# Turning x on VectorE instead of TensorE, in quarter rows with four fetches per tile: lightning attention followed by a mixture of experts

## The chip, the cores and the metric

One core of one Trainium2 chip. The metric is the device time of one execution, in microseconds (us), as a median over executions. The experiments ran in five calls; all kernels of one call ran on the same chip, beside fresh runs of the kernel before.

## The reference, cut to what matters

```python
# attention: B=4, H=8 heads, S=768, D=64, blocks of 64 tokens, decay lam per head
for b in range(nb):
    intra = einsum('bhic,bhjc->bhij', qb, kb) * Dmask;  intra = einsum('bhij,bhjd->bhid', intra, vb)
    inter = einsum('bhid,bhde->bhie', qb * lam_pow, kv_state)
    out[:, :, sl] = intra + inter
    kv_state = lam_block * kv_state + einsum('bhsd,bhse->bhde', kb * rev_pow, vb)
x = out.transpose(0, 2, 1, 3).reshape(B, S, 512)
# experts: E=8, hidden F=1024
for each sequence b, token s:
    fresh_e = argmax(x[b, s] @ w_gate)
    e = fresh_e if s == 0 or local_gate[b, s] < 0.5 else prev_e        # locality
    out[b, s] = softmax(logits)[e] * (relu(x[b, s] @ w1[e]) @ w2[e])
```

Which expert a token takes is known only after its attention, and depends on the tokens before it. So the kernel makes x, routes the 3072 tokens, gathers them by expert into tiles of 128, and runs two matrix products per tile.

## The kernel before

There are 24 attention steps (128 tokens each, numbered 0 to 23), then 24 expert tiles (0 to 23) and some half tiles. Attention leaves x with the features on the partitions (`xc`). The kernel gathers it by token from memory, where it lies with one row per token, and multiplies it by `w1` with the features on the partitions again. So x is turned twice, both times by TensorE, against an identity matrix:

```python
def rows_of(s):                                   # once per attention step
    px = pg.tile([P, DM], F32, name="pk1")
    for a in range(A):                            # A = 4
        nc.tensor.transpose(px[:, P*a:P*a + P], xc[:, a, ORDER[s][0]], ident)
    xn = moe.tile([P, DM], F32, name="xn")
    nc.scalar.copy(xn, px)
    nc.scalar.dma_start(out=x_dram[P*s:P*s + P, :], in_=xn)

def collect(xg, i, j):                            # one tile's 128 tokens, by index: ONE transfer of 256 KB
    nc.gpsimd.indirect_dma_start(out=xg, in_=x_dram[:n, :],
        in_offset=bass.IndirectOffsetOnAxis(ap=gidx[i][:, j:j + 1], axis=0), ...)

def turned(g):                                    # once per expert tile
    pt = pg.tile([P, DT, P], F32, name="po1")
    for d in range(DT):                           # DT = 4
        nc.tensor.transpose(pt[:, d], xgt[g % 2][:, P*d:P*d + P], ident)
    nc.vector.tensor_copy(xtt[g % 2], pt)

def hidden(g, half):                              # 32 matmuls, then one relu on ScalarE
    ...
    nc.scalar.activation(hts[g][:, FT//2*half:FT//2*half + FT//2], ph, ACT.Relu)

# the order of tile 3 (finished(g) is output(g), written(g), weights(g + 2))
        hidden(3, 0)
        hidden(3, 1)
        by_slots(1, (0, 1, 2, 3, 4))              # routing of the later tiles, small matmuls
        turned(4)
        finished(3)
```

`xgt` has two buffers. `written(g)` scales the output on VectorE and scatters it by an indirect transfer that GpSimd issues too, so GpSimd has two transfers per tile. The routing (`fresh_experts` ... `by_slots`) is cut into stages, hung into the attention steps from 9 on (`extras`) and into tiles 0 to 3. The program has TensorE, VectorE and SyncE run in exactly the order written (`tc.manual_schedule(engines={PE, DVE, SP})`).

## Time and profile before

| | value | how to read it |
|---|---|---|
| time | 494.96 us (494.44 to 497.23) | three runs |
| span of the profiled execution | 493.0 us | first to last instruction of the core |
| attention, to the first expert matmul | 106.9 us | timeline: where tile 0's first matmul starts |
| one plain expert tile | 14.45 us | distance of two tiles' first matmuls |
| GpSimd | 106.8 us (22%) | busy time in the page |
| last tile's start to the end | 23.0 us | second product, the last output's scatter and its landing |

A plain tile is 14.45 us of TensorE with nothing between. The attention stage is mixed: there TensorE, VectorE and the loads are all busy for more than half of the time.

### The profile page before, as it was taken

Reading aid. Unit: us, or ns where it says so; the run is one execution under the profiler, and the core shown is the slowest. Engines: PE = TensorE matmul, PEld = TensorE weight load, DVE = VectorE, ACT = ScalarE, POOL = GpSimd, SP = SyncE. Lnnn points to the kernel's source line nnn. Section 1 sums busy time; section 2 is a strip of 40 time slices with the busy share of each in tenths; the row PEclk is TensorE's granted clock in tenths of the full one; section 3 lists DMA queues with packets and bytes.
Section 4 is the critical chain, followed back from the end, with each engine's and each line's share of the span. In section 5 each row is a group of like instructions: output and inputs, shape, how many; then the busy total and the mean of one; then the engine's idle time right before and its main releaser. Section 6 shows DMA issues by size and latency. Waiting matters only on the chain. (4 is left out here: it accounts for less than half of the span.)

```text
span 493.0 us, 10193 instructions
## 1 busy us (share of the span) xinstructions
PE 475.2 (96%) x4231; PEld 351.6 (71%) x4231; DVE 127.3 (26%) x315; ACT 84.7 (17%) x212; POOL 106.8 (22%) x118
## 2 busy tenths in 40 slices
PE   6999999989999999999999999999999999999992
PEld 5877788776777667658657856876667777666770
DVE  6645677652367301011010101101110110110000
ACT  2256656331110000000000001000000000000000
POOL 5575564300101300221011100201101101110000
PEclk9899999999999999999999999999999999999997
DMA  7999999996788999999999997699954980894000
GB/s 272 411 418 380 352 342 330 401 368 233 260 319 292 324 378 399 395 376 397 398 333 386 398 398 277 211 330 319 327 194 157 310 314 31 284 332 169 23 25 17
DMA packets 49850, 146.42 MB, mean 297 GB/s; under 512 B 3244, under 2 KB 3244, under 8 KB 46960
## 3 DMA queue, kind: packets, MB, share of 16 engines
q1 hardware_dynamic: 42096, 125.86, 69.9%
q0 software_dynamic: 4224, 13.37, 7.1%
q10 hardware_dynamic: 3456, 6.29, 3.4%
q8 instruction: 36, 0.59, 0.5%
q14 instruction: 38, 0.31, 0.2%
HBM read 153.90 MB, written 12.98 MB: 338 GB/s over the span
## 5 line engine op out<-in xcount | busy, mean ns | idle before, releaser
L646 PEld LDWEIGHTS ps<-xt,w 128*128 128x128 f32 x1536 | 175.0, 192 | 14.0 <-issue 12.9
L646 PE MATMUL ps<-xt,w 128*128 128x128 f32 x1536 | 177.1, 276 | 0.8 <-DVE xt L631 0.8
L653 PE MATMUL pk<-w,ht 128*128 128x512 f32 x384 | 168.8, 592 | 0.0
L653 PEld LDWEIGHTS pk<-w,ht 128*128 128x128 f32 x384 | 71.1, 190 | 80.4 <-issue 80.4
L648 ACT ACTIVATE ht<-ps 128x512 f32<-128x512 f32 x48 | 28.7, 598 | 314.7 <-PE ps L646 314.2
L659 POOL DMA_INDIRECT out_dram<-y,sidx x24 | 24.6, 1026 | 196.3 <-DVE y L658 179.3
L658 DVE TENSOR_SCALAR y<-pk,gate 128x512 f32<-128x512 f32 x24 | 18.0, 751 | 146.0 <-PE pk L653 140.6
L637 DVE COPY xt<-po 128x512 f32<-128x512 f32 x23 | 15.9, 691 | 143.2 <-PE po L636 143.1
L621 POOL DMA_INDIRECT xg<-x_dram,gidx x24 | 25.0, 1041 | 121.2 <-PE po L636 84.1
L189 DVE TENSOR_TENSOR sm<-ps,mask 128x512 f32<-128x512 f32 x46 | 29.6, 685 | 15.1 <-PE ps L185 15.0
L165 POOL TENSOR_TENSOR qd<-inp,lamq 128x512 f32<-128x512 f32 x20 | 25.6, 1282 | 23.3 <-PE po L212 8.8
L185 PE MATMUL ps<-inp 64*64 64x128 f32 x736 | 26.3, 282 | 2.0 <-DMA inp<-in_qkv_dram 2.0
L225 PE MATMUL po<-sm,inp 128*64 128x128 f32 x384 | 26.9, 284 | 0.3 <-DMA inp<-in_qkv_dram 0.3
L225 PEld LDWEIGHTS po<-sm,inp 128*64 128x64 f32 x384 | 21.1, 140 | 7.5 <-issue 6.6
L168 POOL TENSOR_TENSOR kd<-inp,rev 128x512 f32<-128x512 f32 x20 | 22.4, 1122 | 16.1 <-PE pk L234 7.6
L185 PEld LDWEIGHTS ps<-inp 64*64 64x64 f32 x736 | 20.6, 136 | 5.6 <-issue 4.6
L246 ACT COPY xn<-pk 128x512 f32<-128x512 f32 x24 | 14.1, 588 | 30.6 <-DMA x_dram<-xn 19.8
L216 ACT ACTIVATE kv<-kv,lamq 128x64 f32<-128x64 f32 x64 | 17.1, 337 | 9.8 <-PE po L212 6.4
L228 ACT COPY xc<-po 128x256 f32<-128x256 f32 x48 | 15.3, 371 | 14.2 <-PE po L225 14.0
L244 PE MATMUL pk<-ident,xc 128*128 128x128 f32 x96 | 15.7, 286 | 0.0
L234 PE MATMUL pk<-inp,kd 128*64 128x64 f32 x320 | 13.2, 222 | 1.2 <-issue 1.1
L636 PE MATMUL po<-ident,xg 128*128 128x128 f32 x92 | 13.8, 273 | 0.0
(182 smaller groups left out, 223.6 us busy)
## 6 DMA issues: line engine op xcount, KB each, us to landing
w<-in_w_dram SPq DMA_DIRECT2D x57, 2048.0 KB
inp<-in_qkv_dram SPq DMA_DIRECT2D x22, 1024.0 KB
x_dram<-xn ACTq DMA_DIRECT2D x24, 256.0 KB
inp<-in_qkv_dram SPq DMA_DIRECT2D x4, 512.0 KB
w<-in_w_dram SPq DMA_DIRECT2D x4, 512.0 KB
xg<-x_dram,gidx POOLq DMA_INDIRECT x24, 7.0
out_dram<-y,sidx POOLq DMA_INDIRECT x24, 6.9
xgh<-x_dram,gidx POOLq DMA_INDIRECT x3, 6.4
```

The lines of the kernel that those rows point to most:

```text
L165: nc.gpsimd.tensor_tensor(qd, x[:, 0].rearrange("p (a i) -> p a i", i=P), lamq, ALU.mult)
L168: nc.gpsimd.tensor_tensor(kd.rearrange("p (h d) -> p h d", d=DH), x[:, 2].rearrange("p (h d) -> p h d", d=DH), rev.unsqueeze(2).broadcast_ ...
L185: nc.tensor.matmul(ps[u][js, a], lhsT=kt[rows, a, js], rhs=qt[rows, a], start=True, stop=True, skip_group_check=True)
L189: nc.vector.tensor_tensor(sm[:, u], ps[u], mask[:, u], ALU.mult)
L216: nc.scalar.mul(kv[:, a], kv[:, a], lamq[:, a, P - 1:P])
L225: nc.tensor.matmul(head(a, u), lhsT=vn[:, a, u], rhs=sm[:, u, a], start=(not c and a < 2), stop=True, skip_group_check=True)
L621: nc.gpsimd.indirect_dma_start(out=xg, out_offset=None, in_=x_dram[:n, :], in_offset=bass.IndirectOffsetOnAxis(ap=gidx[i][:, j:j + 1], axi ...
L646: nc.tensor.matmul(ph[:, i], lhsT=w1t[g % 2][:, d, P * f:P * f + P], rhs=xtt[g % 2][:, d], start=(d == 0), stop=(d == DT - 1))
L648: nc.scalar.activation(hts[g][:, FT // 2 * half:FT // 2 * half + FT // 2], ph, ACT.Relu)
L653: nc.tensor.matmul(pys[g % 2], lhsT=ht[:, f], rhs=w2t[g % 2][:, f], start=(f == 0), stop=(f == FT - 1))
L658: nc.vector.tensor_scalar(y, pys[g % 2], gate[i][:, j:j + 1], None, ALU.mult)
L659: nc.gpsimd.indirect_dma_start(out=out, out_offset=bass.IndirectOffsetOnAxis(ap=sidx[i][:, j:j + 1], axis=0), in_=y, in_offset=None, bound ...
```

## The change

The intent is to free TensorE of all transposes of x. VectorE's transpose of a 128x512 tile, from SBUF to SBUF, turns 32x32 blocks and leaves the blocks in their places. A token's row then falls into four quarter rows of 128 values that lie with 32-token groups. So x is kept in memory as quarter rows, each tile's 128 tokens are fetched by four transfers of 64 KB (each with its own column of indices), and one more VectorE transpose brings the features onto the partitions. The routing stages are moved to earlier steps, the last twelve turns of x wait until tiles 1 to 3, and `by_slots(1)` is drawn between the halves of tile 3. The core of the diff:

```diff
 def rows_of(s):
-    for a in range(A):
-        nc.tensor.transpose(px[:, P*a:P*a + P], xc[:, a, ORDER[s][0]], ident)
-    nc.scalar.copy(xn, px)
-    nc.scalar.dma_start(out=x_dram[P*s:P*s + P, :], in_=xn)
+    b, c = ORDER[s]
+    xn = moe.tile([P, Q, A, QP], F32, name="xn", bufs=4)                 # Q = 4, QP = 32
+    nc.vector.transpose(out=xn.rearrange("p c a r -> p a c r"),
+                        in_=xcs[c][:, :, b].rearrange("p a (c t) -> p a c t", t=QP))
+    nc.sync.dma_start(out=x_dram[Q*P*s:Q*P*s + Q*P, :].rearrange("(p c) k -> p c k", c=Q), in_=...)

 def collect(xg, i, j):
-    nc.gpsimd.indirect_dma_start(out=xg, ..., ap=gidx[i][:, j:j + 1], ...)
+    for c in range(xg.shape[1]):                                          # 4, or 2 for a half tile
+        nc.gpsimd.indirect_dma_start(out=xg[:, c], ..., ap=gidx[i][:, j, c:c + 1], ...)

 def turned(g):
-    for d in range(DT):
-        nc.tensor.transpose(pt[:, d], xgt[g % 2][:, P*d:P*d + P], ident)
-    nc.vector.tensor_copy(xtt[g % 2], pt)
+    turn(xtt[g % 2], xgt[g % 2])                                          # one nc.vector.transpose

+def wrapped(i):                       # the quarter rows' indices: two small matmuls per part
+    ...
 extras = {                            # (cut: most routing stages one to three places earlier)
-    (19, 1): by_slots(0, (0, 1)), (20, 0): (ahead(0), ahead(1), rows_out(0)),
+    (18, 1): by_slots(0, (0, 1)), (19, 1): (wrapped(0), ahead(0), ahead(1), rows_out(0)),
 ...
         hidden(3, 0)
+        by_slots(1, (0, 1, 2, 3, 4))
+        for s in range(NA + 8, NT):
+            rows_of(s)
         hidden(3, 1)
-        by_slots(1, (0, 1, 2, 3, 4))
+        wrapped(1)
```

## The prediction

> **What bounds the kernel now.** I read the page's parts 1 and 2 first, then the groups of instructions, then the timeline of one attention step, one expert tile and the stretch where the two stages meet.
>
> ```profile
> PE 475.2 (96%) x4231; PEld 351.6 (71%) x4231; DVE 127.3 (26%) x315; ACT 84.7 (17%) x212; POOL 106.8 (22%) x118
> ...
> PE   6999999989999999999999999999999999999992
> ...
> DVE  6645677652367301011010101101110110110000
> ...
> DMA  7999999996788999999999997699954980894000
> ```
>
> TensorE is busy from the first slice to the last but one. VectorE is 50 to 80% busy in the first quarter only (attention and routing) and nearly idle in the expert tiles. DMA is full in the attention stage and in slices 13 to 23. A TensorE instruction taken away is therefore worth its slot in the queue, unless VectorE (first quarter) or DMA takes over.
>
> ```profile
> L244 PE MATMUL pk<-ident,xc 128*128 128x128 f32 x96 | 15.7, 286 | 0.0
> L636 PE MATMUL po<-ident,xg 128*128 128x128 f32 x92 | 13.8, 273 | 0.0
> L246 ACT COPY xn<-pk 128x512 f32<-128x512 f32 x24 | 14.1, 588 | 30.6 <-DMA x_dram<-xn 19.8
> L637 DVE COPY xt<-po 128x512 f32<-128x512 f32 x23 | 15.9, 691 | 143.2 <-PE po L636 143.1
> L621 POOL DMA_INDIRECT xg<-x_dram,gidx x24 | 25.0, 1041 | 121.2 <-PE po L636 84.1
> L189 DVE TENSOR_TENSOR sm<-ps,mask 128x512 f32<-128x512 f32 x46 | 29.6, 685 | 15.1 <-PE ps L185 15.0
> ```
>
> The first four are what goes. Matmuls are pipelined, so a slot is read from starts, not from durations:
>
> ```profile
> 35.40 0.63 PE L234 MATMUL pk<-inp,kd 128*64 128x64 f32 x16
> ...
> 35.96 0.65 PE L244 MATMUL pk<-ident,xc 128*128 128x128 f32 x4
> ...
> 36.55 1.10 PE L185 MATMUL ps<-inp 64*64 64x128 f32 x32
> ...
> 433.78 0.60 PE L636 MATMUL po<-ident,xg 128*128 128x128 f32 x4
> ...
> 434.22 7.03 PE L653 MATMUL pk<-w,ht 128*128 128x512 f32 x16
> ```
>
> In attention the four transposes hold TensorE from 35.96 to 36.55, 0.59 us of a step of 3.55; in a tile from 433.78 to 434.22, 0.44 us of 14.45.
>
> [...] No transpose of VectorE is in this trace; the 512-element operations [...]are, at 685 and 691 ns, so I estimate 0.70 us for one. [...] a fetch of 256 KB costs POOL 1.04 us to issue and lands after 7.8 to 8.0 us where DMA is full (85 to 112 us). So four fetches are four issues, 4.2 us, and the last lands some 3.2 us later than one did.
>
> **The change, part by part.**
> *Removed from TensorE.* 24 steps of 0.59 = 14.2. The first tile's turn: L630 starts at 105.50, the first expert matmul at 106.88, 1.4 with the wait for its copy. 23 tiles of 0.44 = 10.1. Three half tiles of 0.44 = 1.3. Sum 27.0 us. ScalarE loses 24 copies and the waits for x's writes, off the path.
>
> *Moved to VectorE.* In a tile one 0.69 copy becomes one transpose of about 0.70 that waits for the fetch alone, so it runs some 10 us before it is needed: no cost. In steps 1 to 12 VectorE gets 0.70 more per step; the last twelve transposes run in tiles 1 to 3.
>
> *Charge 1, the first steps.* Before, VectorE in steps 1 to 3 had 3 x (1.29 masks + 0.42 state) and about 4.0 of constants = 9.1 us, and TensorE took 9.3. Now add 3 x 0.70 and nine more small constants at 0.17 to 0.25, about 1.7: 12.9 us, against 3 x 2.52 = 7.6 of TensorE. Here VectorE becomes the bound (loads land only every 3 us there too). Following the order up to step 5, scores of step 6 start at about 29.5, where they start now. The five transposes before that gain nothing: 5 x 0.59 = 2.9.
>
> *Charge 2, routing in the middle.* A step of TensorE is 3.55 - 0.59 = 2.96 (4.9 with gates). VectorE per step, from the rows before plus transpose: steps 9 and 10 3.5, step 12 5.2, step 13 3.6, step 17 4.1, step 18 3.3. Overruns 0.5, 0.5, 0.3, 0.6, 1.1, 0.3 = 3.3. The scores run a step ahead, which absorbs part: 2.0.
>
> *Charge 3, the seam.* Steps 20 to 23 cost TensorE about 4.0 + 2.4 + 2.4 + 1.5 = 10.3. The first tile's indices are known some 0.8 after step 19; the fourth fetch issues 3.2 later, lands 7.9 later, is turned in 0.9: 12.8. Wait 2.5. (VectorE's own work to there, 11.2, and POOL's last qd, behind eight fetches of 1.04, end nearly as late.)
>
> *Charge 4, the third tile.* The matmuls of by_slots for the other tiles move from after the second half of hidden(3) to after its first half. They need five products on VectorE:
>
> ```profile
> 154.11 0.75 DVE L658 TENSOR_SCALAR y<-pk,gate 128x512 f32<-128x512 f32 x1 [2.07 <-PE pk L653]
> 154.78 0.90 DVE L535 TENSOR_TENSOR hit<-whole,to 128x720 bf16<-128x720 f32 x1
> ...
> 155.71 4.18 DVE L544 TENSOR_TENSOR w<-hit,parts 128x720 bf16<-128x720 bf16 x5
> ...
> 160.94 1.68 PEld L554 LDWEIGHTS <-lane 128*128 128x128 bf16 x24
> ```
>
> Today they end at 159.9, TensorE wants them at 160.9: no wait. In the new order VectorE, from the start of tile 2, has y 0.75, the tables and slots 7.9 (143.46 to 151.38), four transposes 2.8, the turn 0.7, the chances 3.1 (moved here): 15.3, past the tile's 14.0. Then y, hit and five products, 5.8: ready 7.1 after tile 3 starts. TensorE asks at 3.6. Wait 3.5.
>
> *Charge 5.* Four small matmuls for the quarter indices and small waits: 0.8.
>
> Sum of charges 2.9 + 2.0 + 2.5 + 3.5 + 0.8 = 11.7. Net 27.0 - 11.7 = 15.3; 494.96 - 15.3 = 479.7, call it 480.
>
> **Rivals.**
> *All 27 us arrive* (468): for it, VectorE stands at 26% and TensorE waits for hardly anything; against it, the step sums of charges 1 and 2 exceed 2.96, and the orders of charges 3 and 4 are fixed. If the transpose is quicker than 0.70 or the single waits overlap, 472.
> *DMA becomes the bound.* For it: the stretch from 172 to 296 us moves 385 GB/s and would have to move about 399 in 120 us; attention in steps 5 to 12 loads 1.05 + 0.26 + 0.13 MB per 3.45 us, 418 GB/s, where the page has 412 to 416 at its best. Against it: queuing each 2 MB weight load at 5.6 us after its issue, it lands 7 to 18 us ahead of its first matmul; loads of q, k and v are issued five steps ahead; 3 MB of x's writes leave the attention stage. I charge nothing beyond charge 1; if wrong, 484 to 486.
> *VectorE's transpose is slow,* say 1.25 us for 32-bit elements. Then steps 1 to 12 carry 6.6 us more on the engine that is already full, most of it on the path, and tile 3 waits 2 more: 487. Nothing in the trace speaks to it[...].
> *POOL becomes the bound in the tiles.* 4.2 + 1.0 of 14.0 us: no. It matters only at the seam.
>
> **Range and chances.** The 27.0 removed is firm to 1 us. The charges are sums of single waits, 6 to 19 us together. 8 in 10: 473 to 487. Faster by over 2% means under 485.1: needs the charges under 17, which I give 0.83. Within 2% 0.16, slower 0.01.
>
> **What would show it.** Right: the rows for L244 and L636 are gone with a tile period of 14.0; a transpose row of about 0.70; TensorE waiting for VectorE masks before step 6 (the same instant as now, near 29.5); a wait of 2 to 3 us before the first expert matmul, ended by the transpose of xt, itself waiting for a fetch; a wait of 3 to 4 us ahead of by_slots in tile 3, ended by the last product. Wrong: transposes over 1 us; TensorE waiting for weights from 170 us on; a tile period still near 14.4; or no wait at the seam or in tile 3, which would make it about 474.

## The result, and the profile after

The first measurement gave 509.54 us (507.78 to 511.4, four runs) against 496.1 us (494.44 to 497.9, four runs) of the kernel before. The ratio is 1.0271, with a 95% interval of 1.0205 to 1.0337: slower. The outputs are right. Ratios here are the mean time of one kernel's fast runs over that of the other's of the same rounds, so they are not quite the ratio of the medians quoted.

The page of that run, in the parts that answer to those shown of before (busy time; slices; then line, engine, operation, count, busy time and mean ns):

```profile
PE 462.5 (91%) x4031; PEld 335.4 (66%) x4031; DVE 151.1 (30%) x354; ACT 72.3 (14%) x188; POOL 181.8 (36%) x193
...
PE   6788988789996985999899999999999999979995
...
L664 DVE STREAM_TRANSPOSE xt<-xg 128x512 f32<-128x512 f32 x24 | 16.9, 703 | 26.6 <-remote 9.9
...
L659 POOL DMA_INDIRECT xg<-x_dram,gidx x96 | 97.0, 1010 | 88.7 <-issue 39.0
```

TensorE did lose its 200 instructions, and a VectorE transpose costs the 0.70 us that was estimated from VectorE's 512-element operations of before (685 and 691 ns). But TensorE's row now has holes (slices 13, 16 and 36; a slice is 12.65 us) where the row before had nines, and a new kind of releaser has appeared, "remote": a signal that the profile could assign to no instruction of this core. The same word stands at tile 20, the place of slice 36 (timeline: start, duration, engine, line, operation, and in brackets the idle time before it and what ended it):

```profile
439.22 7.55 PE L680 MATMUL ps<-xt,w 128*128 128x128 f32 x63
...
446.28 0.60 ACT L682 ACTIVATE ht<-ps 128x512 f32<-128x512 f32 x1 [13.13 <-remote]
...
450.69 1.00 POOL L659 DMA_INDIRECT xg<-x_dram,gidx  x1 [0.30 <-DMA out_dram<-y,sidx]
...
453.46 0.37 SPq L647 DMA_DIRECT2D w<-in_w_dram  x1
453.47 0.60 ACT L682 ACTIVATE ht<-ps 128x512 f32<-128x512 f32 x1 [6.59 <-remote]
...
454.12 3.70 PE L687 MATMUL pk<-w,ht 128*128 128x512 f32 x8 [2.68 <-ACT ht L682]
```

ScalarE applies relu to the first 32 matmuls of the tile, which by the record ended at 442.95, and it starts at 446.28; to the second 32, which ended at 447.86, and it starts at 453.47. Nothing was in its way. SyncE, whose weight load also waits for those matmuls, is let go in the same hundredth of a microsecond as ScalarE (453.46). TensorE then waits 2.68 us for the relu. All through this GpSimd issues transfers with 0.30 us between them: this tile's fetches, the next tile's and a scatter, twelve in a row, the last at 450.69.

I call *lateness* the time from the recorded end of a half tile's last matmul to the start of its relu. It is 0.04 to 0.12 us in nearly every half tile of every kernel (up to 0.31 in the kernel before). I leave out the first half of tile 0, where ScalarE still has attention work before it (4.45 us in the kernel before). Of the other 47 halves, ten were over 0.5 us late in the changed kernel's first run, up to 9.59 us, and their lateness adds up to 29.9 us. In the tables below, sums are of what exceeds the usual amount.

### The profile page after: what moved, and what is told of

It is laid out like the page before. It is cut to its first block, busy times and chain, and to the rows that moved or that the text cites.

```text
span 506.1 us, 10011 instructions
## 1 busy us (share of the span) xinstructions
PE 462.5 (91%) x4031; PEld 335.4 (66%) x4031; DVE 151.1 (30%) x354; ACT 72.3 (14%) x188; POOL 181.8 (36%) x193
## 5 line engine op out<-in xcount | busy, mean ns | idle before, releaser
L680 PEld LDWEIGHTS ps<-xt,w 128*128 128x128 f32 x1536 | 177.3, 193 | 17.9 <-issue 17.6
L680 PE MATMUL ps<-xt,w 128*128 128x128 f32 x1536 | 180.4, 277 | 4.1 <-issue 4.0
L687 PE MATMUL pk<-w,ht 128*128 128x512 f32 x384 | 171.5, 598 | 8.9 <-ACT ht L682 7.7
L659 POOL DMA_INDIRECT xg<-x_dram,gidx x96 | 97.0, 1010 | 88.7 <-issue 39.0
L191 PE MATMUL ps<-inp 64*64 64x128 f32 x736 | 29.7, 282 | 7.9 <-DMA inp<-in_qkv_dram 2.3
L195 DVE TENSOR_TENSOR sm<-ps,mask 128x512 f32<-128x512 f32 x46 | 29.5, 681 | 6.5 <-PE ps L191 6.4
L191 PEld LDWEIGHTS ps<-inp 64*64 64x64 f32 x736 | 22.3, 136 | 12.4 <-issue 5.8
L664 DVE STREAM_TRANSPOSE xt<-xg 128x512 f32<-128x512 f32 x24 | 16.9, 703 | 26.6 <-remote 9.9
L218 PE MATMUL po<-qd,kv 64*64 64x128 f32 x320 | 16.3, 280 | 3.9 <-issue 3.6
L218 PEld LDWEIGHTS po<-qd,kv 64*64 64x64 f32 x320 | 12.3, 136 | 5.4 <-issue 5.3
L251 DVE STREAM_TRANSPOSE xn<-xc 128x512 f32<-128x512 f32 x24 | 15.8, 683 | 0.0
```

Source lines behind the costliest of these rows:

```text
L191: nc.tensor.matmul(ps[u][js, a], lhsT=kt[rows, a, js], rhs=qt[rows, a], start=True, stop=True, skip_group_check=True)
L195: nc.vector.tensor_tensor(sm[:, u], ps[u], mask[:, u], ALU.mult)
L218: nc.tensor.matmul(head(a, u), lhsT=kv[rows, a], rhs=qd[rows, a], start=(a < 2), stop=False, skip_group_check=True)
L659: nc.gpsimd.indirect_dma_start(out=xg[:, c], out_offset=None, in_=x_dram[:n, :], in_offset=bass.IndirectOffsetOnAxis(ap=gidx[i][:, j, c:c ...
L680: nc.tensor.matmul(ph[:, i], lhsT=w1t[g % 2][:, d, P * f:P * f + P], rhs=xtt[g % 2][:, d], start=(d == 0), stop=(d == DT - 1))
L687: nc.tensor.matmul(pys[g % 2], lhsT=ht[:, f], rhs=w2t[g % 2][:, f], start=(f == 0), stop=(f == FT - 1))
```

## The experiments

The theory after the first result: GpSimd's transfers in a row hold up the signals of other engines. Its rivals: the transfers' data traffic or small pieces (DMA) do it; VectorE's transpose does it; or the new order of the routing.

### First call (chip 14): the fetches alone, and the fetches thinned

**b_four**: the kernel before, with its fetch in four pieces of 512 bytes per token, all else untouched.

```diff
-nc.gpsimd.indirect_dma_start(out=xg, ..., ap=gidx[i][:, j:j + 1], ...)
+for c in range(0, xg.shape[1], P):
+    nc.gpsimd.indirect_dma_start(out=xg[:, c:c + P], ..., ap=gidx[i][:, j:j + 1], element_offset=c, ...)
```

> The kernel before with one thing of the change: each gather of token rows is made as four fetches of 512 B a row (column quarters of the same row) in place of one of 2 KB; the turns stay on TensorE, the routing stays where it was. Train theory (long unbroken runs of fetches on GpSimd, 1.0 us each, hold up the other engines): the fetches of tiles 0 and 1, of tiles 5, 6, 7 with the first half tile, and those after the two program switches become trains of 8 to 13, and the time rises by 8 to 18 us, to 504 to 514 us, with single stalls of 2 to 9 us at the same tiles as in the changed kernel. Rival ([...] fetches are hidden): within 2 us of before, 494 to 498 us.

Measured: 495.17 us (494.12 to 498.61), ratio 1.0006 (0.9943 to 1.0069). It has up to 17 transfers in a row and no late signal: the largest lateness is 0.12 us. That is the outcome of the rival in which the fetches are hidden, on this chip.

**a_single**: the changed kernel with one fetch of 2 KB per token instead of four of 512 bytes. Its output is wrong, which doesn't matter for the time. A token gets the four quarter rows that lie together in memory, the work is the same but for one small VectorE addition.

```diff
-for c in range(xg.shape[1]):
-    nc.gpsimd.indirect_dma_start(out=xg[:, c], in_=x_dram[:n, :], ..., ap=gidx[i][:, j, c:c + 1], ...)
+nc.gpsimd.indirect_dma_start(out=xg.rearrange("p c k -> p (c k)"),
+                             in_=x_dram.rearrange("(n c) k -> n (c k)", c=Q), ..., ap=gone[i][:, j:j + 1], ...)
```

> The changed kernel with one fetch of 2 KB per row in place of the four of 512 B (whole quarter-row groups at the index of the token, so the rows that arrive are the wrong ones and the result is wrong on purpose; bytes, waits, turns on VectorE and routing are as in the changed kernel; one small VectorE add more). Train theory: the stalls at steps 20 to 21 and at tiles 4, 7 and 20 go, 509.5 falls by 17 to 25 us to 485 to 493 us; the wait of tile 3 and the slow attention steps stay. Rival [...]: 505 to 510 us, the stalls at tiles 4, 7 and 20 stay.

Measured: 488.1 us (487.66 to 490.7), ratio 0.9865 (0.9812 to 0.9918). No late signal.

**b_train**: the kernel before, with 8 and 16 transfers into a tile that nothing reads, added to two expert tiles.

```diff
+for k in range({GB: 8, GB + 2: 16}.get(g, 0)):
+    nc.gpsimd.indirect_dma_start(out=junk[:, k], ..., ap=gidx[1][:, 0:1], element_offset=P * (k % 4), ...)
```

> The kernel before with idle fetches added on GpSimd in two undisturbed tiles, each of 128 rows of 512 B into a buffer that nothing reads: 8 in a row at the start of tile 14 and 16 in a row at the start of tile 16. Train theory, if the length of the train alone does it: tile 14 or 15 grows from 14.45 us by 2 to 5 us, tiles 16 and 17 together by 6 to 12 us, with signals of TensorE that reach the other engines only when the train ends. Rival (the trains only go with the stalls, whose cause is the weights' transfers, the program switch or the half tiles beside them): all of tiles 14 to 18 stay at 14.45 us within 0.3.

Measured: 497.84 us, one run. GpSimd's order is not fixed by the program: the scheduler drew all 24 dummies forward to 168 to 201 us, so the two tiles meant to suffer show nothing, and the test as planned failed. But it made the longest series, 30 transfers with under 0.8 us between them, and lateness stayed at 0.12 us or less.

**a_gate**: the changed kernel, with a tiny GpSimd product ahead of some groups of fetches, which reads the relu's output of an earlier tile, so that a group of four can't start before it.

```diff
+def after(xg, at):
+    nc.gpsimd.tensor_tensor(xg[0:1, :, 0], at[:, :xg.shape[1]], at[:, :xg.shape[1]], ALU.mult)
 ...
-ahead(6)
 hidden(4, 0)
+ahead(6, hts[4][0:1, 0, 0:Q])
```

> The changed kernel with the same fetches, but broken into groups of four (two for a half tile): before each group a GpSimd product of 1x4 elements that reads what ScalarE wrote at a chosen place (first or second half of the tile that runs), so that a group of fetches starts only then; tile 1 is fetched after step 21, tile 6 after half of tile 4, tile 7 after half of tile 5, and so on. Train theory: the stalls at step 21, tile 4, tile 7 and tile 20 (6, 9, 3 and 4 us) mostly go: 487 to 496 us. Rival (the number of fetches, their small packets or VectorE are what costs, not their order): 505 us or more; a third, late fetches: new waits of VectorE for a fetch before a turn, at the tiles that are gated.

Measured: 492.19 us (490.28 to 494.72), ratio 0.9931 (0.987 to 0.9992). No late signal. A half tile's fetch now comes late and its tile waits for it (tile 8 takes 23.81 us).

My reading then was that four fetches are harmless in the kernel before, and that thinning them takes about 17 us off the changed kernel, so that trains and the VectorE transpose must act together. That reading compared these runs on chip 14 with a first result from a chip that is not recorded. It did not hold.

### Second call (chip 5): which partner does the train need

**b_fourturn**: b_four with `turned` on VectorE (wrong values, since blocks stay in place). **a_pe**: the changed kernel with the expert tiles' turns back on TensorE (wrong values). **a_act**: the changed kernel with x's writes issued by ScalarE again. **a_rows**: the changed kernel whose four fetches take a token's four quarters of one row, so pieces of 512 bytes that lie together (wrong values).

```diff
 # b_fourturn, on b_four
-for d in range(DT): nc.tensor.transpose(pt[:, d], xgt[g % 2][:, P*d:P*d + P], ident)
-nc.vector.tensor_copy(xtt[g % 2], pt)
+nc.vector.transpose(out=xtt[g % 2] (p c d t), in_=xgt[g % 2] (p c d r))
 # a_pe, on the changed kernel, tiles from 1 on
-turn(xtt[g % 2], xgt[g % 2])
+for d in range(DT): nc.tensor.transpose(pt[:, d], xgt[g % 2][:, d], ident)
+nc.vector.tensor_copy(xtt[g % 2], pt)
 # a_act
-nc.sync.dma_start(out=x_dram[...], in_=xn)
+nc.scalar.dma_start(out=x_dram[...], in_=xn)
 # a_rows
-in_=x_dram[:n, :], ap=gidx[i][:, j, c:c + 1]
+in_=x_dram.rearrange("(n c) k -> n (c k)", c=Q), ap=gone[i][:, j:j + 1], element_offset=P * c
```

> The kernel before with four fetches of 512 B per tile (which cost nothing alone: 495.2 us) and with the turn of each full tile on VectorE (one transpose of 128x512 in 32x32 blocks in place of four on TensorE and a copy; the rows are not cut for it, so the result is wrong on purpose). x writes and routing as before. If trains of fetches harm only where VectorE reads the fetched tile itself: stalls of 2 to 9 us at tiles 4 to 7 and behind the second program switch, 495 us or more. If not: the 23 turns of 0.44 us come off TensorE, 10 us, to 485 us within 2, and no tile longer than before's except tile 5.

> The changed kernel with the turns of full tiles 1 to 23 back on TensorE (four transposes and a copy from PSUM; tile 0, half tiles and x itself stay on VectorE; the values are in the wrong order, so the result is wrong on purpose). Fetches, trains, x writes and routing stay. If the stalls need VectorE as the reader of the fetched tile: they go at tiles 4, 7 and 20 (15 us), the turns come back (10 us): 503 to 506 us. If not: the stalls stay and 10 us are added: 517 to 521 us.

> The changed kernel with the writes of x given to ScalarE's DMA queue, as before, in place of SyncE's, which also carries all weights. If the stalls come of SyncE's queue (a write that waits for VectorE keeps the weights behind it back, or 512 B pieces beside the weights): step 21 and tile 4 lose 6 and 9 us of excess, 494 to 500 us. If not: 507 to 512 us with the same stalls.

> The changed kernel with the same four fetches of 512 B per tile, but each taking a column quarter of the token's own 2 KB row (a wrong result on purpose), so that the four fetches of a tile read neighbouring addresses as in the kernel before with four fetches, which had trains of 17 without a stall. If the spread addresses of quarter rows are what stalls: 487 to 493 us. If not: 507 to 512 us, stalls at step 21 and tiles 4, 7 and 20 as in the changed kernel.

| | us (range, 2 runs each) | ratio | largest lateness | sum of lateness |
|---|---|---|---|---|
| b_fourturn | 514.29 (513.38 to 515.2) | 1.0358 | 12.39 | 23.9 |
| a_pe | 510.84 (508.46 to 513.22) | 1.0289 | 5.26 | 11.2 |
| a_act | 512.18 (512.1 to 512.25) | 1.0316 | 7.00 | 30.2 |
| a_rows | 508.15 (506.95 to 509.36) | 1.0235 | 8.41 | 29.0 |

All four are slower than the kernel before (for a_pe and a_rows it is unclear whether by more than 2%), and all four have late signals. Neither another place for the pieces (a_rows, 29.0 us of lateness) nor another engine for x's writes (a_act, 30.2) took it away: the first result had 29.9. a_pe keeps late signals in tiles 4 and 20, where full tiles are no longer turned on VectorE, but only three over 0.5 us instead of ten, and its 510.84 us lies between the two outcomes that were expected. b_fourturn alone seemed to convict the transpose, since b_four had run at 495 us; but between those two there is a change of chip as well. Nothing measured so far could separate the two.

### Third call (chip 14): the same kernels again

**after_again**, **b_four_again** and **a_gate_again** are unedited repeats. **a_slots** is the changed kernel with `by_slots(1)` put back to its old place, to measure the wait in tile 3.

```diff
 hidden(3, 0)
-by_slots(1, (0, 1, 2, 3, 4))
 for s in range(NA + 8, NT): rows_of(s)
 hidden(3, 1)
+by_slots(1, (0, 1, 2, 3, 4))
 wrapped(1)
```

> The changed kernel, not edited. The runs so far fall in two groups by the chip that they ran on (a number that each result lists), not only by their edits: on chip 14 no signal of TensorE was late in any trace, on chip 5 it was in all four. If the chip or its state decides: here, beside the kernel with four fetches in the order before, either both are without stalls (this one then 490 to 495 us) or both have them. If the program decides: this one is at 508 to 511 us with 4 to 10 us stalls at tiles 4 and 20 whatever the chip.

> The kernel before with four fetches per tile, not edited since its first run (495.2 us, no stall, longest train 17). If the chip decides, it now has the state of its neighbours in this call: 495 us where the changed kernel too has no stall, or 503 us and more where the changed kernel has them. If the program decides: 494 to 498 us while the changed kernel of this call is at 508 to 511.

> The changed kernel with the fetches in gated groups of four, not edited since its first run (492.2 us). If breaking up the trains is what cured it: 490 to 495 us again, also where the changed kernel beside it shows its stalls. If it was only the chip: near the changed kernel of this call, within 4 us.

> The changed kernel with the twelve products that give tiles 5 and up their slots put back behind the second half of tile 3, where they stood before (the x turns stay between the halves). The wait of 3.9 us in the middle of tile 3 and the half-speed TensorE behind it go: tile 3 falls from 21.5 us to 15.5 to 17, and the kernel is 4 to 6 us below the changed kernel of this call. Rival: VectorE is the bound there and the wait only moves behind the second half: under 2 us.

Measured, against 495.33 us of the kernel before: after_again 486.14 us (484.88 to 487.33), ratio 0.9828 (0.9785 to 0.9871); b_four_again 496.99, ratio 1.0048; a_gate_again 492.77, ratio 0.9963; a_slots 484.04 (483.22 to 484.85), ratio 0.9786 (0.9737 to 0.9836). None of the four has a late signal. For a_slots 4 to 6 us were expected; its median is 2.1 us lower, and its tile 3 takes 18.08 us where 15.5 to 17 were expected.

This overturns the first reading. The changed kernel, byte for byte that of the first result, takes 486 us on chip 14. The gates did not cure it there, they cost it over 6 us; and a_single's ratio (0.9865) is no better than that of the unedited kernel, so four fetches instead of one cost nothing in sum on this chip. By the profiles they cost at the start and gain at the end: tile 0 starts at 104.40 us in a_single and at 107.13 and 106.22 us in after_again and after_third, but the stretch from the last tile's start to the end is 23.02 us in a_single and 20.47 and 20.44 in the other two.

### Fourth call (chip 14): a cure prepared

**after_third** and **b_four_third** are unedited repeats. **a_pairs** is a_slots with the fetches in pairs and a gate ahead of each pair, so that no more than two fetches, or a scatter and two fetches, are asked for at once. One pair waits for the second half's relu, the other for the scaled output `y`.

```diff
-def collect(xg, i, j):
+def collect(xg, i, j, cs, mark):
+    if mark is not None:
+        nc.gpsimd.tensor_tensor(xg[0:1, cs[0]:cs[-1] + 1, 0], mark, mark, ALU.mult)
-    for c in range(xg.shape[1]):
+    for c in cs:
 ...
-ahead(g + 2)
 hidden(g, 0)
 hidden(g, 1)
+ahead(g + 2, 0, ht_mark(g, 1))
 ...
-written(g)
+ahead(g + 2, 1, written(g))           # written returns y[0:1, 0:2]
```

> The changed kernel, not edited, a third time, to tell which state this chip is in. Either 485 to 488 us with every first half of a tile signalled to ScalarE within 0.1 us (as on chip 14), or 507 to 512 us with signals 3 to 10 us late at tiles 4 and 20 (as in its first run).

> The kernel before with four fetches per tile, not edited. On a chip where the changed kernel is at 485 to 488: 495 to 497 us again, which tells nothing new. On a chip where the changed kernel is at 507 to 512: if long trains of fetches alone bring the late signals there, this one has them too, in its train of 17 at tiles 4 to 5, and is at 503 to 515 us; if it needs the turns on VectorE as well, 494 to 498 us.

> The changed kernel with the twelve slot products of tile 3 back behind its second half, and no more than three GpSimd transfers in a row: every tile's four fetches are gated as two pairs (a GpSimd product of 1x2 elements that reads what ScalarE or VectorE has just written), a half tile's two fetches stand alone, a scatter of results goes with one pair. In the traces with late signals none came in the first three transfers of a train. If the length of the train is the condition: 483 to 488 us on either kind of chip. If on a chip with late signals it is not the length: 500 us or more beside the changed kernel's 507 to 512. Rival on either: a pair comes late and VectorE waits for it, one or two tiles over 16 us.

Measured, against 493.72 us: after_third 486.83 us (486.04 to 487.63), ratio 0.9862 (0.9776 to 0.9948); b_four_third 494.94, ratio 1.0026; a_pairs 481.83 (480.06 to 483.6), ratio 0.9761 (0.9646 to 0.9875).

The profile of after_third can be laid beside that of the first result: the same program, in the same tile, at the same distance from the tile's start. First tile 17 in the first result:

```profile
397.18 7.31 PE L680 MATMUL ps<-xt,w 128*128 128x128 f32 x64
...
403.70 1.00 POOL L659 DMA_INDIRECT xg<-x_dram,gidx  x1 [0.30 <-issue]
...
405.56 0.60 ACT L682 ACTIVATE ht<-ps 128x512 f32<-128x512 f32 x1 [3.95 <-PE ps L680]
```

and tile 17 in after_third, on chip 14:

```profile
379.81 7.31 PE L680 MATMUL ps<-xt,w 128*128 128x128 f32 x64
...
386.31 0.99 POOL L659 DMA_INDIRECT xg<-x_dram,gidx  x1 [0.30 <-issue]
...
387.15 0.60 ACT L682 ACTIVATE ht<-ps 128x512 f32<-128x512 f32 x1 [2.92 <-PE ps L680]
```

The 64 matmuls take 7.31 us in both, and the fifth transfer of a row starts 6.5 us into the tile in both. The second relu starts 7.34 us after the tile's start on chip 14, at once when the matmuls end, and 8.38 us in the first result, after the transfer has been issued. Nothing in the program differs.

### Fifth call (chip 1): a chip not used yet

**a_pairs_again**, **after_fourth** and **b_four_fourth** are unedited repeats of a_pairs, the changed kernel and b_four.

> The version in pairs (481.8 us on chip 14), not edited. On chip 14: 480 to 484 us again. On a chip where the changed kernel beside it has late signals: 480 to 488 us if short trains avoid them, 495 us or more if not.

> The changed kernel, not edited, to tell the state of this chip: 485 to 488 us without late signals, or 507 to 512 us with them.

> The kernel before with four fetches per tile, not edited. Without late signals in the changed kernel of this call: 494 to 497 us. With them: 503 to 515 us if trains alone bring them, 494 to 498 us if the turns on VectorE are needed too.

Measured, against 494.46 us of the kernel before (494.08 to 498.3): after_fourth 516.71 us (516.38 to 517.04), ratio 1.0432 (1.0343 to 1.0521); b_four_fourth 515.18 (514.91 to 515.44), ratio 1.0401 (1.0313 to 1.049); a_pairs_again 484.19 (480.97 to 488.65, five runs, of which the slowest, the profiled one, is slow), ratio 0.9762 (0.9671 to 0.9853).

b_four decides between the theories. It has no transpose on VectorE and no new order; its only change is four fetches for one. It runs at 495 to 497 us on chip 14 and at 515 us here. Tile 4 of b_four on chip 14:

```profile
171.37 7.39 PE L647 MATMUL ps<-xt,w 128*128 128x128 f32 x64
...
175.29 0.60 ACT L649 ACTIVATE ht<-ps 128x512 f32<-128x512 f32 x1 [12.06 <-PE ps L647]
```

and the same tile of b_four_fourth, on chip 1:

```profile
177.19 1.00 POOL L622 DMA_INDIRECT xgh<-x_dram,gidx  x1 [0.30 <-issue]
...
178.05 0.27 PE L647 MATMUL ps<-xt,w 128*128 128x128 f32 x1 [0.49 <-issue]
...
185.32 0.60 ACT L649 ACTIVATE ht<-ps 128x512 f32<-128x512 f32 x1 [21.16 <-remote]
```

On chip 14 the relu starts 0.10 us after the first half's last matmul. On chip 1 that half ended at 176.11 and the relu starts at 185.32, 9.21 us later. In that train TensorE has gaps of its own too, marked "issue", in which by the profile it waits for nothing. The tile took 23.43 us instead of 14.53.

Lateness of the relu misses the larger half. The profile of b_four_fourth is 20.2 us longer than that of b_four; tile 4 takes 8.9 us more and tile 7 takes 11.2 us more, and in tile 7 no relu is late. There a row of 17 transfers runs from 219.86 to 241.82 us, and from 234 to 244 us TensorE starts only 11 matmuls, up to 1.9 us apart, where 0.11 us is usual:

```profile
234.27 1.00 POOL L622 DMA_INDIRECT xgh<-x_dram,gidx  x1 [0.30 <-issue]
...
234.94 0.27 PE L647 MATMUL ps<-xt,w 128*128 128x128 f32 x1 [0.93 <-issue]
...
236.37 0.27 PE L647 MATMUL ps<-xt,w 128*128 128x128 f32 x1 [1.16 <-issue]
...
244.39 0.48 DVE L829 TENSOR_SCALAR y<-po,gateh 128x256 f32<-128x256 f32 x1 [14.16 <-remote]
```

VectorE's scaling of the half tile's output waits too: the last matmul for it ended at 233.04 us, 11.35 us before (0.07 in b_four). No transfer of instructions starts between 229.4 and 260.4 us in the trace, so it does not show TensorE waiting for its program.

a_pairs_again is 6% faster than the unedited kernel on the same chip, with the same fetches in the same pieces of 512 bytes (moving `by_slots(1)` back, which it also does, was worth 2.1 us in a_slots on chip 14). What is left in its tiles is telling. In tile 4 GpSimd had fallen behind, the gates were already open, and seven transfers follow each other with only the 0.19 us products between:

```profile
179.04 1.00 POOL L661 DMA_INDIRECT xg<-x_dram,gidx  x1 [0.30 <-issue]
...
180.06 0.19 POOL L659 TENSOR_TENSOR xg<-ht 1x2 f32<-1x2 f32 x1
...
180.52 1.00 POOL L661 DMA_INDIRECT xg<-x_dram,gidx  x1 [0.27 <-POOL xg L659]
...
183.88 0.60 ACT L687 ACTIVATE ht<-ps 128x512 f32<-128x512 f32 x1 [4.56 <-remote]
```

The relus of this tile are 1.33 and 2.91 us late, on chip 1 only; one more, in tile 13, is 0.61 late, again in the fifth transfer of a row. So the product without a pause does not cure it. a_pairs on chip 14 has nine in a row there, and is not late. These late relus cost little: this profile, of the slow run, is 5.1 us longer than that of a_pairs, and 3.9 of it lie before tile 0 and had built up before the first fetch.

### All profiles in one table

For each profile: the largest lateness and the sum over the 47 halves of what exceeds the usual amount, with the longest row of GpSimd transfers (under 0.8 us from one to the next). a_act and a_rows stand in the table of the second call; a_single, a_gate, a_gate_again and a_slots, all on chip 14, have no late signal with 4, 9, 9 and 15 in a row.

| kernel | chip | longest row | largest lateness, us | sum, us | time, us |
|---|---|---|---|---|---|
| before | not recorded | 3 | 0.31 | 0.2 | 494.96 |
| b_four, b_four_again, b_four_third | 14 | 17 | 0.12 | 0 | 495.17, 496.99, 494.94 |
| b_train | 14 | 30 | 0.12 | 0 | 497.84 |
| after_again, after_third | 14 | 15 | 0.12 | 0 | 486.14, 486.83 |
| a_pairs | 14 | 9 | 0.12 | 0 | 481.83 |
| after (first result) | not recorded | 15 | 9.59 | 29.9 | 509.54 |
| a_pe | 5 | 13 | 5.26 | 11.2 | 510.84 |
| b_fourturn | 5 | 17 | 12.39 | 23.9 | 514.29 |
| after_fourth | 1 | 15 | 7.69 | 29.4 | 516.71 |
| b_four_fourth | 1 | 17 | 9.21 | 9.2 | 515.18 |
| a_pairs_again | 1 | 7 | 2.91 | 4.8 | 484.19 |

Where lateness occurs at all, a signal over 0.5 us late was always due behind the third transfer of a row (most often in the fifth or sixth), at the latest 1.3 us behind the row's end; those due in the first three transfers are under 0.5 us late. In the same profiles, a_pairs_again excepted, TensorE's own matmuls in tiles 4 and 7 (in four of them in tile 20 too) start more than 0.3 us apart with nothing between, which adds 0.9 to 9.4 us to a tile; in the profiles without late signals it adds 0.2 us at most. What is shown: long rows of GpSimd transfers delay TensorE's signals (by up to 12.39 us) and its matmuls (up to 1.9 us apart in b_four_fourth) in some conditions and not in others (0.12 us at most on chip 14, with up to 30 in a row), they do so without any VectorE transpose in the kernel (b_four_fourth, 9.21 us), and breaking the rows takes nearly all of it away (on chip 1 the sum falls from 29.4 to 4.8 us). What stays open: what the condition is. Chips 1 and 5 were used in one call each, chip 14 in four, so a chip can't be told from its session or its neighbours' load. Open too is what holds the signals and the matmuls physically. The ends of matmuls are modelled in the records, so lateness could in principle be partly TensorE finishing later than recorded; those who wait for it are late in either case.

## Why the prediction was right or wrong

The prediction said 480 us, range 473 to 487. The first result was 509.54. The same program on chip 14 was 486.1 and 486.8.

**The step that failed.** It is this rival and its dismissal: "*POOL becomes the bound in the tiles.* 4.2 + 1.0 of 14.0 us: no. It matters only at the seam." The arithmetic of busy time was right (GpSimd went from 106.8 to 181.8 us, still 36%), and on chip 14 the conclusion was right too. But it asked only whether GpSimd has time enough, not what its rows of transfers do to others. Between the first result's profile and after_third, 506.1 − 484.3 = 21.8 us, the difference lies in few places: tile 0 starts 5.3 us later (one attention step, from 20 to 21, lasts 10.98 us instead of 3.08 while eight fetches are issued), tile 4 takes 9.6 more, tile 7 3.15 more and tile 20 4.43 more, together 22.5 of the 21.8; the other tiles take back 0.7. That it was the rows, b_four_fourth and a_pairs_again show on chip 1; the first result has the same pattern in the same tiles, but its chip is not known. That it appears only in some conditions, no profile of the kernel before could have shown, since that kernel has never more than three in a row.

**The rest, without the late signals.** Here after_third (span 484.3) is compared with the profile before (493.0): 8.7 us gained where 15.3 were predicted.

*The tiles: right.* A plain tile takes 14.01 us; 14.0 was said. A transpose takes 683 ns (of x) or 703 ns (of a fetched tile) on average; 0.70 was said. The rival of a slow transpose, to which nothing in the trace before spoke, is dead. Four fetches of 64 KB land 5.5 us (median) after their issue in after_third, one of 256 KB 7.0 us in the kernel before. Tiles 4 to 22 gain 8.87 us and tiles 0 to 2 gain 1.91.

*Charges 1 to 3, the attention stage and the seam: mis-sized.* 14.2 + 1.4 us of transposes left this stage and 7.4 were charged against them. Tile 0 starts only 0.66 us sooner, so the charges were 14.2 + 1.4 − 0.7 = 14.9. Charge 1 held in this profile: the scores of step 6 start at 29.15 us, 29.45 before, about 29.5 said. So the miss lies in steps 6 to 23, some 12 us where charges 2 and 3 had 4.5. (In after_again the same scores start at 32.98 us, and the later steps lose less.) The mechanism named was right, VectorE becoming the bound; its row in a middle stretch, first before and then after_third (window, its length, then TensorE, weight load, VectorE, ScalarE, GpSimd busy with counts, granted clock, DMA share, GB/s):

```profile
60.00:77.00 17.00, 15.85 (x347) 12.95 (x342) 11.49 (x27) 9.62 (x31) 9.69 (x8) 1.00 0.95 342
```

```profile
60.00:77.00 17.00, 14.79 (x338) 11.96 (x334) 14.04 (x32) 7.29 (x28) 9.55 (x9) 1.00 0.94 349
```

VectorE rose by 2.55 us and TensorE fell by 1.06, in 17 us: TensorE now waits. What I missed is that VectorE's operations had no fixed length here. A small VectorE operation that started 0.05 us after GpSimd's product of q with the decay ended only just after it, in after_third:

```profile
47.92 1.28 POOL L171 TENSOR_TENSOR qd<-inp,lamq 128x512 f32<-128x512 f32 x1 [0.82 <-DMA inp<-in_qkv_dram]
...
47.97 1.30 DVE L370 TENSOR_TENSOR top<-lt,mx 128x64 f32<-128x64 f32 x1
```

The same line on 96 columns took 0.26 us; here, on 64 columns, it takes 1.30 and ends 0.07 us after the product. What lengthened it is not shown. Counting VectorE operations that end within 0.08 us of such a product (or of that of k beside it) and are over 0.3 us longer than their line's shortest, the time lost between 20 and 105 us is 1.7 us before and 5.8 us in after_third. That could account for 4.1 us of the missing 7.5; but the same count gives 2.8 us in after_again, whose tile 0 starts 0.9 us later, and no run removed it, so this is an argument, not shown. The seam wait of 2.5 us was not where it was put: the first expert matmul waits 0.17 us for its transpose, but step 23 waits 1.42 us for GpSimd's last product of q behind the eight fetches, which the prediction had named in brackets.

*Charge 4, tile 3: right in kind, low in size.* A wait of 3.5 us was said, ended by the last of the five products. (VectorE was not "nearly idle in the expert tiles" to begin with: slices 12 and 13 of the row that the prediction quotes, over tiles 2 and 3, show 6 and 7 tenths; this charge counts on it.) In after_third:

```profile
154.69 4.18 DVE L566 TENSOR_TENSOR w<-hit,parts 128x720 bf16<-128x720 bf16 x5
...
158.93 3.16 PE L576 MATMUL pr<-w,lane 128*128 128x150 bf16 x24 [3.86 <-DVE w L566]
...
161.88 3.96 PE L680 MATMUL ps<-xt,w 128*128 128x128 f32 x32
```

and with `by_slots(1)` back in its old place, in a_slots:

```profile
158.52 1.76 PE L576 MATMUL pr<-w,lane 128*128 128x150 bf16 x24 [0.28 <-DVE w L566]
```

The wait is 3.86 us, and then the 24 small matmuls take 3.16 us instead of 1.76. After the wait TensorE runs at half clock: between 159 and 161 us of after_third the granted clock is 0.50, from 161 to 163 0.69, then 1.00; over the same matmuls in the kernel before (160 to 162 us) it is 1.00. So tile 3 costs 5.34 us more than before; a_slots takes 3.4 us off the tile (18.08 against 21.47 in after_again, of the same call) and 2.1 us off the median.

*Not predicted:* from the last tile's start to the end the kernel gains 2.57 us (20.44 against 23.01), since the last scatter lands sooner. It goes with the four fetches: a_single, with one, has 23.02 again, and b_four, the kernel before with four, has 21.19. Why stays open.

*The rival that DMA becomes the bound* is ruled out on chip 14: plain tiles run at 14.01 us without waits for weights. (The 418 GB/s that it asked for are also the most that the page of before shows in a slice; the 412 to 416 of the prediction are from longer windows.)

In sum on chip 14: of the 27.0 us removed, 14.9 and 5.3 went to charges that were put at 7.4 and 3.5; the tiles' small rest (11.4 us removed there, 1.91 + 8.87 seen) is 0.6 where charge 5 said 0.8; the end gave 2.6. 27.0 − 14.9 − 5.3 − 0.6 + 2.6 = 8.8, the 8.7 of the spans within rounding.

**A version that beats both.** a_pairs took 481.83 us on chip 14 and 484.19 us on chip 1 (482.69 without the slow run), 0.9761 and 0.9762 of the kernel before by fast runs. The intervals (up to 0.9875 and 0.9853) leave open whether the gain exceeds 2%.

## What to carry to other kernels

An engine that is far from busy can still hurt: GpSimd is busy for 37% of the span of b_four_fourth, which took 515.18 us where the kernel before took 494.46. Ask not only how long GpSimd's transfers take, but how many stand in a row, and put pauses between them when splitting one transfer into several (on chip 1, a_pairs_again took 484.19 us and the changed kernel 516.71). Before explaining a difference, run the unedited kernel again in the same call as the experiment and, if you can, on another chip (the changed kernel took 486.14 us on chip 14 and 516.71 on chip 1). When work moves to VectorE beside GpSimd's products, allow for operations like the one in after_third that took 1.30 us and ended with such a product, where the same line took 0.26 us on more columns. And don't draw a wait like the 3.86 us of tile 3 into a full TensorE queue: in after_third the granted clock was 0.50 after it, and 24 matmuls took 3.16 us instead of 1.76.
